# Two-level products in part of the gate and value stage of a retention and SwiGLU kernel

## The chip, the cores and the metric

One core of one Trainium2 chip runs the kernel. The time is the device time of one execution in microseconds; the median of several executions is compared. Names of engines: PE is TensorE (matmuls), PEld its weight loads, DVE is VectorE, ACT is ScalarE, POOL is GpSimd, SP is SyncE, which issues nearly all transfers.

## The reference

The inputs are q, k, v of 8 batches, 8 heads, 576 positions and 64 channels, and the weights of a gated feed-forward layer for 4608 tokens with 512 channels and 1536 inner ones. All arithmetic is in float32.

```python
scores = scale * np.matmul(q, k.transpose(0, 1, 3, 2))
ret = scores * Dmat[None]                 # causal decay, gamma by head
x = np.matmul(ret, v)                     # then (B,H,S,D) -> (4608, 512)
...
xn = x / np.sqrt(np.mean(x * x, -1, keepdims=True) + 1e-06) * rms_g
g = xn @ w_gate                           # 512 -> 1536
val = xn @ w_val                          # 512 -> 1536
out = (g / (1 + np.exp(-g)) * val) @ w_out   # 1536 -> 512
```

## The kernel before

**Units.** The 4608 tokens are worked on in nine units of 512 tokens, u = 0 to 8. The first two are mixed with the reading and joining of the weights under a plan written out by hand; units 2 to 8 run in a loop at the end of the kernel. Each has a gate and value stage, in which the 12 chunks of 128 inner channels of both gate and value are formed and multiplied into `h`, and an output stage (`across`), in which `h` meets `w_out`. While a unit's gate and value stage runs, units 2 to 6 also carry the retention of the next tokens (`prepare`, `fetch`, `slot`); from unit 7 on nothing of that is left.

**Groups.** The gate and value stage has six groups, n = 0 to 5: an even n is a gate group, an odd n the value group for the same channels. A group multiplies 512 channels by 512 inner channels (4 chunks, two in the upper half of `h` and two in the lower) for 512 tokens. It does so in the manner of Strassen and Winograd, by 7 products of halves instead of 8: the generator `up` (line 693 on) forms each product as four matmuls of 128 x 128 weights against 256 tokens and yields after each. Of the seven products, the first and fourth gather in the PSUM bank x, the second in y, the third and sixth in z, the fifth and seventh in w; eight banks rotate. The sums of weights that the seven products need were formed at the start and lie in DRAM (`w_up_blocks`, seven blocks a group); the sums of x are formed on DVE by `sums_of_x` (line 611) in the output stage before. The sums of results are left to DVE: with `u2` = x + y and `u4` = u2 + z and so on, five additions a group, each with one input in PSUM. A gate group ends in four Silu on ACT, a value group in four multiplications on DVE into `h`, and in `differences` (line 781), two subtractions that the output stage needs.

**The output stage** has two levels already: 7 products, each of 7 inner products of quarters with 3 matmuls of 128 x 128 against 128 columns (line 872). Its inner sums of `h` are formed by `inner_sums` (line 817) on POOL, in the second part of the tile `vi` (`inner`) and in `sums_x`; the first ones are put on POOL's queue in group 4, the rest when the stage begins. Results are gathered in the first part of `vi` (`vec`), joined by `combine` (seven additions on POOL, line 1061) when the stage is done, and stored by `store` (eight transfers on SP's queue) in group 1 of the next unit.

**Weights.** A ring of 17408 words a partition holds the weights in turn, one piece for each group (3584 words, 1792 KB in all) and one for each output product (2688 words, 1344 KB). `refill` (line 652) sends the next pieces on SP's queue as soon as the room they want is free; `used`, which the last product of a piece calls, triggers it. All instructions of an engine run in the order in which the program writes them (`manual_schedule`); between engines only the semaphores of the data decide.

Of the kernel before, what the change touches and what calls it, by code (L numbers as in the profile page):

```python
# [10 lines left out]
F32 = mybir.dt.float32  # L11
U32 = mybir.dt.uint32
AF = mybir.ActivationFunctionType
ALU = mybir.AluOpType
P = 128
# [29 lines left out]
def kernel(  # L45
# [11 lines left out]
    nc = tc.nc  # L57
# [3 lines left out]
    NHP = H // 2  # L61
# [16 lines left out]
    assert S == U + L and NU == B + 1 and NK == 3 and NG == 3  # L78

    const = ctx.enter_context(tc.tile_pool(name="const", bufs=1))  # L80
    raw = ctx.enter_context(tc.tile_pool(name="raw", bufs=1))
    att = ctx.enter_context(tc.tile_pool(name="att", bufs=2))
    xp = ctx.enter_context(tc.tile_pool(name="xp", bufs=3))
    tmp = ctx.enter_context(tc.tile_pool(name="tmp", bufs=4))
    PS = bass.MemoryType.PSUM
    dram = ctx.enter_context(tc.tile_pool(name="dram", bufs=1, space=bass.MemoryType.DRAM))
    banks = ctx.enter_context(tc.tile_pool(name="banks", bufs=8, space=PS))

    def bank(name):
        return banks.tile([P, 512], F32, tag="b", name=name)  # L90
# [4 lines left out]
    def row(name):  # L95
        return tmp.tile([P, U], F32, tag="n", name=name, bufs=3)
# [443 lines left out]
    def same_rows():  # L540

        t = tmp.tile([P, SQ], F32, tag="d", name="d", bufs=1)
        nc.vector.tensor_reduce(
            out=t, in_=ident.rearrange("p (a b) -> p b a", b=SQ), axis=mybir.AxisListType.X,
            op=ALU.add,
        )
        nc.vector.tensor_copy(
            out=alike.rearrange("p (a b) -> p a b", b=SQ),
            in_=t.unsqueeze(1).to_broadcast([P, P // SQ, SQ]),
        )  # L550
# [73 lines left out]

    UP, OUT = 7 * 2 * 2 * P, 7 * NK * P
    w_up_d = dram.tile([2 * NG, P, UP], F32, name="w_up_blocks")
    w_out_d = dram.tile([7, NK, P, 7 * P], F32, name="w_out_blocks")
    FIRST_ORDER = (A11, S4, A12, S1, S2, S3, A22)  # L630
# [7 lines left out]
    pieces = [("out", 0, n) for n in range(7)] + [("out", 1, n) for n in range(4, 7)]  # L638
    N_FIRST = len(pieces)
    for u in range(2, NU):  # L640
        pieces += [("up", u, n) for n in range(2 * NG)] + [("out", u, n) for n in range(7)]
    places = []
    at = AT_SUMS
    for kind, u, n in pieces:
        size = UP if kind == "up" else OUT
        if at + size > RING:
            at = AT_SETS if kind == "out" and u < 2 else 0
        places.append((at, at + size))
        at += size
    n_sent = n_used = 0  # L650

    def refill(most=len(pieces)):

        nonlocal n_sent
        while n_sent < min(most, len(pieces)):
            a, z = places[n_sent]
            kind, u, n = pieces[n_sent]
            if any(a < y and x < z for x, y in places[n_used:n_sent]):
                return
            if u > 1 and n_used < N_FIRST and a < NF * U:  # L660
                return
            o = ring[:, a:z]
            if kind == "up":
                src = w_up_d[n]
            else:
                o = o.rearrange("p (c x) -> p c x", c=NK)
                src = w_out_d[order_of(u)[n]].rearrange("c p x -> p c x")
            nc.sync.dma_start(out=o, in_=src)
            n_sent += 1

    def piece(kind, u, n):
        if kind == "out" and u == 1 and n < 4:
            i = pieces.index(("out", 0, n + 3))
        else:
            i = pieces.index((kind, u, n))
        assert i < n_sent and (i == n_used or kind == "out" and u == 0)
        a, z = places[i]
        if kind == "up":
            return ring[:, a:z].rearrange("p (b c f) -> p b c f", b=7, c=2)
        return ring[:, a:z].rearrange("p (c n d) -> p n c d", n=7, c=NK)  # L680

    def used():
        nonlocal n_used
        n_used += 1
        refill()
# [7 lines left out]
    def up(u, n):  # L693


        m, f = n % 2, n // 2 * 2
        w = piece("up", u, n)

        def product(blk, ps, start):
            for i in range(2):  # L700
                for c in range(2):
                    nc.tensor.matmul(  # L702
                        ps[:, i * HU : i * HU + HU], lhsT=w[:, PLACE[blk], c, i * P : i * P + P],
                        rhs=t_of[u][blk][:, c], start=(start and i == c == 0), stop=False,
                        skip_group_check=True,
                    )
# [36 lines left out]
        result(f, 1, "c12", u2, z)  # L743
        yield
        product(A22, w_, False)
        used()
        result(f + NH, 0, "c21", u2, w_)
        if m:
            differences(u, f)
        yield  # L750

    def up_plain(u, k, n):
# [28 lines left out]
    def differences(u, f):  # L781

        hh = h_1 if u == 1 else h
        b11, b12, b22 = hh[:, f : f + 2, :HU], hh[:, f : f + 2, HU:], hh[:, NH + f : NH + f + 2, HU:]
        for o, a, b in ((t1_of(u)[:, f : f + 2], b12, b11), (b12, b22, b12)):
            nc.vector.tensor_tensor(out=o, in0=a, in1=b, op=ALU.subtract)
# [52 lines left out]
    def across(u):  # L839
# [148 lines left out]
        for n, nm in enumerate(banks_in_turn):  # L988
# [66 lines left out]
                if n in ahead:  # L1055
                    inner_sums(u, ahead[n])
            yield
        if u and not last:
            combine(slice(0, 4), nc.gpsimd)

    def combine(b, eng=nc.vector, late=False):
# [273 lines left out]

    with tc.manual_schedule():
        start()
        for u in range(2, NU):  # L1340
            j0 = NHP * (u + 1)
            more = u + 1 < B
            for n in range(2 * NG):
                for i, _ in enumerate(up(u, n)):
                    if n == 1 and i == 4:
                        store(u - 1)
                    if n == 2 * NG - 2 and i == 1:
                        inner_sums(u, 0, 0)
                        inner_sums(u, 1, 0)
                    if more and i == 2 and 0 < n <= NHP:  # L1350
                        if j0 + n < len(jobs):
                            prepare(j0 + n)
                            fetch(j0 + n + 1)
                    if u + 1 < NU and n == 2 * NG - 1:
                        if i < NHP:
                            gather(u + 1, i, square(u + 1, i))
                        elif i == NHP:
                            fold(u + 1)
                        elif i == 6:
                            meet(u + 1)  # L1360
                    if (u, n, i) == (2, 2, 1):
                        same_rows()
                    if more and (n, i) == (NHP, 5) and j0 + NHP == len(jobs):
                        values(j0 + NHP - 1)
                if more and n <= NHP and (n or u == 2):
                    if j0 + n < len(jobs):
                        slot(j0 + n, rest=(n > 0))
                    else:
                        carried(j0 + n - 1)
            for i, _ in enumerate(across(u)):  # L1370
                if u + 1 == NU:
                    continue
                if i == 2:
                    root(u + 1)
                elif i in (3, 4, 5, 6):
                    scale_x(u + 1, (i - 3,))
                elif i == 8:
                    sums_of_x(u + 1)
# [27 lines left out]
```

## Time and profile before

| | |
|---|---|
| median of 3 runs | 1101.41 us (1101.27 to 1105.15) |
| profiled execution | 1100.22 us, its span 1098.4 us |
| TensorE clock granted | 0.997 of full speed |
| busy in the span: PE, DVE, POOL, ACT | 99%, 66%, 40%, 30% |
| gate and value stage of unit 7, of unit 8 | 883.25 to 955.90, 988.82 to 1061.35 |
| output stage of unit 7 | 955.90 to 988.82 |
| ring loads: 1792 KB, 1344 KB, issue to landing | 7.7 us, 6.4 us (medians) |
| HBM | 220 GB/s over the span |

Times inside the execution count from the start of the span. In rows of groups the first number is the summed busy time and the second the mean of one in ns; "idle before" is how long the engine stood still before such instructions, and what ended that. A matmul of float32 appears as two records.

### The profile page before, as it was taken

What the parts mean: (1) busy time and instruction counts of PE and PEld (TensorE: products, weight loads), DVE (VectorE), ACT (ScalarE), POOL (GpSimd) and SP (SyncE); (2) the same over time, 40 slices, a digit from 0 to 9 for tenths busy, and PEclk for the clock granted to TensorE, in tenths of its full rate; (3) what the DMA queues carried; (4) which work ended last, traced back from release to release, by engine and by line L of the source; (5) the groups of instructions that cost most, each with busy time, mean ns of one, the idle gap of its engine ahead of it and who ended that gap; (6) DMA issues with size and microseconds to landing.
All of it is one profiled execution on the core that took longest, in us unless ns stands there. A gap on an engine that the chain in (4) does not pass through costs nothing.

```text
span 1098.4 us, 24471 instructions
## 1 busy us (share of the span) xinstructions
PE 1085.5 (99%) x10102; PEld 912.2 (83%) x10102; DVE 727.2 (66%) x1251; ACT 328.2 (30%) x739; POOL 443.8 (40%) x421
## 2 busy tenths in 40 slices
PE   9899999999999999999999999999999999999998
PEld 7744444479988899889988998899888988998898
DVE  3878468877866774677667855677565735674467
ACT  5755564331124412332034203330233111201110
POOL 0026326538430195027702571237321932383236
PEclk9999999999999999999999999999999999999999
DMA  8756787596978876797678865888475755585471
GB/s 210 178 190 235 297 252 214 194 354 176 292 276 226 221 256 225 185 240 241 245 217 200 290 257 148 243 255 291 136 204 198 280 194 174 195 287 160 146 250 42
DMA packets 253871, 243.60 MB, mean 222 GB/s; under 512 B 193216, under 2 KB 213824, under 8 KB 247616
## 3 DMA queue, kind: packets, MB, share of 16 engines
q1 hardware_dynamic: 252320, 241.64, 69.7%
q8 instruction: 79, 1.29, 0.5%
q10 hardware_dynamic: 1440, 0.40, 0.2%
q14 instruction: 32, 0.26, 0.1%
HBM read 211.92 MB, written 30.08 MB: 220 GB/s over the span
## 4 chain that ended last, share of the span: by engine, by line
PE 97%; DVE 1%; issue 1%; ACT 0%; POOL 0%; POOLq 0%; DVEq 0%; ACTq 0%
PE up L762 15%; PE x L702 14%; PE w L702 13%; PE z L702 13%; PE y L702 7%; PE xo L872 6%; PE xp L872 4%; PE zo L872 4%; PE zp L872 3%; PE wo L872 2%; PE yo L872 2%; PE av L382 2%; PE av L402 2%; PE wp L872 2%; PE s L295 2%; PE yp L872 2%
## 5 line engine op out<-in xcount | busy, mean ns | idle before, releaser
L762 PE MATMUL up<-x,ring 128*128 128x512 f32 x384 | 167.1, 594 | 0.0
L702 PE MATMUL x<-x,ring 128*128 128x256 f32 x672 | 161.0, 382 | 0.0
L702 PE MATMUL w<-sums,ring 128*128 128x256 f32 x672 | 158.9, 379 | 0.0
L702 PE MATMUL z<-x,ring 128*128 128x256 f32 x672 | 158.7, 379 | 0.0
L824 POOL TENSOR_TENSOR vi<-h 128x384 f32<-128x384 f32 x32 | 42.4, 1326 | 275.9 <-DVE h L721 266.4
L762 PEld LDWEIGHTS up<-x,ring 128*128 128x128 f32 x384 | 72.2, 190 | 89.3 <-issue 84.7
L702 PEld LDWEIGHTS z<-x,ring 128*128 128x128 f32 x672 | 127.7, 190 | 17.4
L702 PEld LDWEIGHTS w<-sums,ring 128*128 128x128 f32 x672 | 127.6, 190 | 17.4
L702 PEld LDWEIGHTS x<-x,ring 128*128 128x128 f32 x672 | 125.3, 190 | 17.5 <-ACT m L728 0.2
L829 POOL TENSOR_TENSOR vi<-h 128x384 f32<-128x384 f32 (+2 forms) x46 | 43.9, 954 | 149.2 <-DVE h L721 149.2
L1068 POOL TENSOR_TENSOR vi<-vi 128x512 f32<-128x512 f32 (+1 forms) x77 | 78.2, 1028 | 51.9 <-DVE vi L899 35.5
L702 PE MATMUL y<-sums,ring 128*128 128x256 f32 x336 | 79.4, 379 | 0.0
L728 ACT COPY m<-x 128x512 f32<-128x512 f32 x42 | 24.6, 587 | 173.3 <-PE x L702 173.3
L709 DVE TENSOR_TENSOR h<-u,w 128x512 f32<-128x512 f32 x42 | 28.9, 688 | 67.8 <-PE w L702 67.8
L702 PEld LDWEIGHTS y<-sums,ring 128*128 128x128 f32 x336 | 63.8, 190 | 8.7
L709 DVE TENSOR_TENSOR u<-m,y 128x512 f32<-128x512 f32 x42 | 28.8, 686 | 63.2 <-PE y L702 62.5
L723 ACT ACTIVATE h<-h 128x512 f32<-128x512 f32 x63 | 39.7, 629 | 83.3 <-DVE h L709 83.3
L1188 POOL TENSOR_TENSOR vi<-vi 128x512 f32<-128x512 f32 (+1 forms) x24 | 40.7, 1696 | 30.4 <-DVE vi L1177 16.9
L709 DVE TENSOR_TENSOR u<-u,z 128x512 f32<-128x512 f32 x42 | 28.9, 687 | 33.6 <-PE z L702 33.4
L1188 POOL TENSOR_TENSOR ring<-ring 128x512 f32<-128x512 f32 x24 | 30.4, 1273 | 49.6 <-DMA w_up_blocks<-ring 43.9
L426 ACT COPY x<-av 128x192 f32<-128x192 f32 (+6 forms) x136 | 37.8, 278 | 30.0 <-PE av L402 28.5
L829 POOL TENSOR_TENSOR vi<-h,vi 128x384 f32<-128x384 f32 (+2 forms) x46 | 44.5, 968 | 3.6
(327 smaller groups left out, 2039.2 us busy)
## 6 DMA issues: line engine op xcount, KB each, us to landing
ring<-w_out_blocks SPq DMA_DIRECT2D x59, 1344.0 KB, 6.4
ring<-w_up_blocks SPq DMA_DIRECT2D x42, 1792.0 KB, 7.7
w_out_blocks<-vi SPq DMA_DIRECT2D x21, 448.0 KB, 6.2
out_dram<-vi SPq DMA_DIRECT2D x64, 128.0 KB, 3.1
qraw<-in_q_dram SPq DMA_DIRECT2D x96, 72.0 KB, 4.7
kraw<-in_k_dram SPq DMA_DIRECT2D x96, 72.0 KB, 2.7
k<-in_k_dram SPq DMA_DIRECT2D x48, 128.0 KB, 2.8
v<-in_v_dram SPq DMA_DIRECT2D x48, 128.0 KB, 3.1
```

What stands on the lines that cost most here:

```text
L295: nc.tensor.matmul(s[e][side(odd), i * L : i * L + L], lhsT=d["kT"][side(e), c * L : c * L + L], rhs=d["qT"][side(e), c * L : c * L + L], ...
L426: nc.scalar.copy(out=o, in_=part)
L702: nc.tensor.matmul(ps[:, i * HU : i * HU + HU], lhsT=w[:, PLACE[blk], c, i * P : i * P + P], rhs=t_of[u][blk][:, c], start=(start and i == ...
L709: nc.vector.tensor_tensor(out=o, in0=a, in1=pairs_of(ps), op=ALU.add)
L723: nc.scalar.activation(out=o, in_=c, func=AF.Silu)
L728: nc.scalar.copy(out=s1, in_=pairs_of(x_))
L762: nc.tensor.matmul(ps, lhsT=w[:, PLACE[blk], c % 2, i * P : i * P + P], rhs=x_of[u][:, c], start=(c == 0), stop=(c == NHP - 1),)
L824: eng.tensor_tensor(out=i1, in0=x12, in1=x11, op=ALU.subtract)
L829: eng.tensor_tensor(out=o[:, c], in0=a[:, c], in1=b[:, c], op=op)
L872: nc.tensor.matmul(ps, lhsT=lhs[:, c], rhs=w[:, s, c], start=((nm, s // 4) not in first), stop=False, skip_group_check=True,)
L1068: eng.tensor_tensor(out=t[:, :, o], in0=t[:, :, x], in1=t[:, :, y], op=ALU.add)
L1188: nc.gpsimd.tensor_tensor(out=t[o], in0=t[x], in1=t[y], op=op)
```

## The change

In the last two units (`LATE`, u = 7 and 8), groups n = 1, 2 and 3 (`DEEP`, "groups 2 to 4" counted from one) use two levels: `up_deep` takes each of the seven products apart into seven products of quarters, 49 matmuls of 128 x 128 weights against 128 tokens instead of 28 against 256. Such a product needs two banks, so a group uses all eight. The inner sums of weights are formed by `inner_blocks` on POOL, one group in each of units 3, 4 and 5, from the piece that lies in the ring, and stored by seven transfers to the new DRAM tensor `w_in_blocks`; `saves` spreads these over SP's queue. In units 7 and 8 these groups load both tensors, in two pieces a group (`HALVES`, 4096 and 3072 words) and three transfers a piece. The inner sums of x are formed on DVE in group 0 by `inner_x` (eight operations). The sums of products are kept as seven parts (`deep_c`), joined by `combine_in` (seven operations of 512 elements on POOL) after the group, and only then multiplied or put through Silu: these ends are kept in `unfinished` and run in the next groups, those of group 3 in groups 4 and 5 (`FINISH`). The pools of the retention are closed in unit 7, and `deep_c` takes their room.

Other things move: in units 7 and 8 `combine` of the unit before is written in group 1 instead of at the end of its output stage, and `store` in group 2 instead of group 1; the first `inner_sums` of units 3 to 8 are written in group 5 instead of group 4, after all saves.

```diff
-    raw = ctx.enter_context(tc.tile_pool(name="raw", bufs=1))
-    att = ctx.enter_context(tc.tile_pool(name="att", bufs=2))
     xp = ctx.enter_context(tc.tile_pool(name="xp", bufs=3))
     tmp = ctx.enter_context(tc.tile_pool(name="tmp", bufs=4))
+    retention = ctx.enter_context(ExitStack())
+    raw = retention.enter_context(tc.tile_pool(name="raw", bufs=1))
+    att = retention.enter_context(tc.tile_pool(name="att", bufs=2))
...
-    UP, OUT = 7 * 2 * 2 * P, 7 * NK * P
+    UP, OUT, IN = 7 * 2 * 2 * P, 7 * NK * P, 7 * P
+    HALVES = (0, 4), (4, 7)
+    DEEP = range(1, 4)
+    LATE = (NU - 2, NU - 1)
+    IN_ORDER = (A11, S1, S2, S3, A12, A22, S4)
+    USED_IN = (A11, S2, S1, S3), (A12, S4, A22)
...
+    assert NHP * (LATE[0] + 1) >= len(jobs)
+    w_in_d = dram.tile([len(DEEP), P, 7 * 4 * P], F32, name="w_in_blocks")
...
-        pieces += [("up", u, n) for n in range(2 * NG)] + [("out", u, n) for n in range(7)]
+        for n in range(2 * NG):
+            if u in LATE and n in DEEP:
+                pieces += [("in", u, (n, i)) for i in range(2)]
+            else:
+                pieces.append(("up", u, n))
+        pieces += [("out", u, n) for n in range(7)]
...
-        size = UP if kind == "up" else OUT
+        size = {"up": UP, "out": OUT}.get(kind)
+        if kind == "in":
+            size = (HALVES[n[1]][1] - HALVES[n[1]][0]) * 8 * P
...
+            elif kind == "in":
+                i, z = HALVES[n[1]]
+                o = o.rearrange("p (b k x) -> p b k x", k=2, x=4 * P)
+                src = w_up_d[n[0]].rearrange("p (b x) -> p b x", b=7)
+                for x, y in spans_of(IN_ORDER[i:z]):
+                    nc.sync.dma_start(
+                        out=o[:, x : x + len(y), 0], in_=src[:, y[0] : y[0] + len(y)]
+                    )
+                src = w_in_d[n[0] - DEEP[0]].rearrange("p (b x) -> p b x", b=7)[:, i:z]
+                o = o[:, :, 1]
...
+    PARTS = (A12, S4, A22, S3, A11, S2, S1)
+    ENDS = (0, 0), (1, 1), (0, 1), (1, 0)
+    deep_u = [
+        vi[:, NV + i * IN : NV + i * IN + IN].rearrange("p (s t) -> p s t", s=7) for i in range(2)
+    ]
...
+    def inner_blocks(u, n):
+        w = piece("up", u, n).rearrange("p b c f -> p b (c f)")
+        d = w_in_d[n - DEEP[0]]
+        t6 = vi[:, NV : NV + 6 * 4 * P].rearrange("p (b s f) -> p b s f", b=6, s=4)
+        t1_ = row(f"inner_{n}").rearrange("p (b s f) -> p b s f", b=1, s=4)
+        for t, b in ((t6, slice(0, 6)), (t1_, slice(6, 7))):
+            a11, a21, a12, a22 = (w[:, b, i * P : i * P + P] for i in range(4))
+            s1, s2, s3, s4 = (t[:, :, i] for i in range(4))
+            for o, x, y, op in (
+                (s3, a11, a21, ALU.subtract), (s1, a21, a22, ALU.add),
+                (s2, s1, a11, ALU.subtract), (s4, a12, s2, ALU.subtract),
+            ):
+                nc.gpsimd.tensor_tensor(out=o, in0=x, in1=y, op=op)
+        def save(i):
+            b = PLACE[IN_ORDER[i]]
+            t = t6[:, b] if b < 6 else t1_[:, 0]
+            nc.sync.dma_start(
+                out=d[:, i * 4 * P : i * 4 * P + 4 * P], in_=t.rearrange("p s f -> p (s f)")
+            )
+        saves.extend(lambda i=i: save(i) for i in range(7))
...
+    def inner_x(u, part):
+        if not deep_x1:
+            retention.close()
+            late = ctx.enter_context(tc.tile_pool(name="late", bufs=1))
+            deep_c.extend(late.tile([P, 4, 7, P], F32, name=f"deep_c_{i}") for i in range(2))
+            deep_x2.append(late.tile([P, 4, 3, P], F32, name="deep_x2"))
+            deep_x1.append(
+                xp.tile([P, NHP, U], F32, tag="x", name="inner_x")
+                .rearrange("p k (a t h) -> p k a t h", a=2, t=2)
+            )
+        x = x_of[u].rearrange("p (a c) (t s h) -> p c s a t h", c=2, t=2, s=2)
+        y = sums_x.rearrange("p i c (s h) -> p c s i h", s=2)
+        for o, v_ in (((deep_x1[0], x), (deep_x2[0], y))[part],):
+            t1_, t3, t2, t4 = (o[:, i] for i in range(4))
+            x11, x12, x21, x22 = v_[:, 0, 0], v_[:, 0, 1], v_[:, 1, 0], v_[:, 1, 1]
+            for r, a, b, op in (
+                (t1_, x12, x11, ALU.subtract), (t3, x22, x12, ALU.subtract),
+                (t2, t3, x11, ALU.add), (t4, x21, t2, ALU.subtract),
+            ):
+                nc.vector.tensor_tensor(out=r, in0=a, in1=b, op=op)
...
+    def up_deep(u, n):
+        m, f = n % 2, n // 2 * 2
+        c, first = deep_c[n % 2], deep_u[n % 2]
...
+        def product(blk, nm, start):
+            half = int(blk in USED_IN[1])
+            w = piece("in", u, (n, half))[:, IN_ORDER.index(blk) - HALVES[half][0]]
+            if start:
+                held_in[nm] = bank(f"{nm}o_{u}_{n}"), bank(f"{nm}p_{u}_{n}")
+            for i, s in enumerate(PARTS):
+                nc.tensor.matmul(
+                    held_in[nm][i // 4][:, i % 4 * P : i % 4 * P + P], lhsT=w[:, IN_AT[s]],
+                    rhs=moving(blk, s), start=(start and i % 4 == 0), stop=False,
+                    skip_group_check=True,
+                )
+            if blk == USED_IN[half][-1]:
+                used()
...
+        def copy(o, nm):
+            for t, ps in halves_of(o, nm):
+                nc.scalar.copy(out=t, in_=ps)
+        def add(o, a, nm):
+            for (t, ps), (x, _) in zip(halves_of(o, nm), halves_of(a, nm)):
+                nc.vector.tensor_tensor(out=t, in0=x, in1=ps, op=ALU.add)
+        def combine_in(which):
+            at = PARTS.index
+            for o, x, y in (
+                (A12, A11, A12), (A11, A11, S2), (S1, A11, S1), (S4, S1, S4), (A11, A11, S3),
+                (S3, S1, S3), (A22, A11, A22),
+            ):
+                nc.gpsimd.tensor_tensor(
+                    out=c[:, which, at(o)], in0=c[:, which, at(x)], in1=c[:, which, at(y)],
+                    op=ALU.add,
+                )
+        def result(i):
+            a, t = ENDS[i]
+            o = h[:, f + a * NH : f + a * NH + 2, t * HU : t * HU + HU]
+            x = c[:, i, :4].rearrange("p s t -> p (s t)").rearrange("p (f t) -> p f t", f=2)
+            if m:
+                nc.vector.tensor_tensor(out=o, in0=o, in1=x, op=ALU.mult)
+            else:
+                nc.scalar.activation(out=o, in_=x, func=AF.Silu)
...
+        def finish(n_=1):
+            for _ in range(max(0, min(n_, len(unfinished)))):
+                unfinished.pop(0)()
+        product(A11, "x", True)
+        copy(first, "x")
+        yield
+        product(S2, "y", True)
+        add(first, first, "y")
+        if m:
+            finish(len(unfinished) - 4)
+        yield
+        product(S1, "z", True)
+        add(c[:, C22], first, "z")
+        yield
+        product(S3, "w", True)
+        add(c[:, C22], c[:, C22], "w")
+        yield
+        product(A12, "x", False)
+        copy(c[:, C11], "x")
+        if m:
+            finish(len(unfinished))
+        split = n == DEEP[-1] and not m
+        if split:
+            combine_in(slice(0, 2))
+        yield
+        product(S4, "z", False)
+        add(c[:, C12], first, "z")
+        if not m:
+            finish()
+        yield
+        product(A22, "w", False)
+        add(c[:, C21], first, "w")
+        if not m:
+            finish()
+        combine_in(slice(2 * split, 4))
+        ends = [lambda i=i: result(i) for i in range(4)]
+        if m:
+            ends[:2] = [lambda: (result(C11), result(C22))]
+            ends[1:] = [lambda: (result(C12), result(C21)), lambda: differences(u, f)]
+        unfinished.extend(ends)
         yield
...
-        if u and not last:
+        if u and not last and u + 1 not in LATE:
             combine(slice(0, 4), nc.gpsimd)
...
+    z = DEEP[-1]
+    FINISH = {(z + 1, 5): 1, (z + 1, 6): 1, (z + 2, 1): 1} if z % 2 else {(z + 1, 1): 3, (z + 1, 4): 2}
...
-                for i, _ in enumerate(up(u, n)):
-                    if n == 1 and i == 4:
+                deep = u in LATE and n in DEEP
+                if u == n + 2 and n in DEEP:
+                    inner_blocks(u, n)
+                for i, _ in enumerate((up_deep if deep else up)(u, n)):
+                    if saves and (n > NHP - 1 or i % 2) and (u != n + 2 or i > 4):
+                        saves.pop(0)()
+                    if u in LATE and n == 0 and i in (0, 2):
+                        inner_x(u, i // 2)
+                    if u in LATE and (n, i) == (1, 0):
+                        combine(slice(0, 4), nc.gpsimd)
+                    if i == 4 and n == (2 if u in LATE else 1):
                         store(u - 1)
-                    if n == 2 * NG - 2 and i == 1:
+                    if (n, i) == ((2 * NG - 1, 2) if u >= DEEP[0] + 2 else (2 * NG - 2, 1)):
+                        while saves:
+                            saves.pop(0)()
                         inner_sums(u, 0, 0)
                         inner_sums(u, 1, 0)
...
+                    for _ in range(FINISH.get((n, i), 0) if u in LATE else 0):
+                        unfinished.pop(0)()
...
```

More of the change, by code (lines that the diff above doesn't have):

```diff
@@ L623, in sums_of_x, with spans_of @@
         t_of[u] = {A11: b11, A12: b21, S1: b12, A22: t4, S2: t2, S3: t3, S4: b22}
-    UP, OUT = 7 * 2 * 2 * P, 7 * NK * P
+    UP, OUT, IN = 7 * 2 * 2 * P, 7 * NK * P, 7 * P
[4 more added lines that the diff above has]
+    USED_IN = (A11, S2, S1, S3), (A12, S4, A22)
+    def spans_of(blocks):
+        spans = []
+        for i, b in enumerate(blocks):
+            if spans and spans[-1][1][-1] + 1 == PLACE[b]:
+                spans[-1][1].append(PLACE[b])
+            else:
+                spans.append((i, [PLACE[b]]))
+        return spans
+    assert NHP * (LATE[0] + 1) >= len(jobs)
+    w_in_d = dram.tile([len(DEEP), P, 7 * 4 * P], F32, name="w_in_blocks")
     w_up_d = dram.tile([2 * NG, P, UP], F32, name="w_up_blocks")
@@ L679, in piece @@
             return ring[:, a:z].rearrange("p (b c f) -> p b c f", b=7, c=2)
+        if kind == "in":
+            return ring[:, a:z].rearrange("p (b s f) -> p b s f", s=8, f=P)
         return ring[:, a:z].rearrange("p (c n d) -> p n c d", n=7, c=NK)
@@ L749, in up @@
             differences(u, f)
+        yield
+    PARTS = (A12, S4, A22, S3, A11, S2, S1)
+    ENDS = (0, 0), (1, 1), (0, 1), (1, 0)
+    C11, C22, C12, C21 = range(4)
+    deep_c = []
+    deep_x2 = []
+    deep_u = [
+        vi[:, NV + i * IN : NV + i * IN + IN].rearrange("p (s t) -> p s t", s=7) for i in range(2)
+    ]
+    deep_x1 = []
+    unfinished, saves = [], []
+    IN_AT = {A11: 0, A12: 2, A22: 3, S1: 4, S2: 5, S3: 6, S4: 7}
+    def inner_blocks(u, n):
[18 more added lines that the diff above has]
+        saves.extend(lambda i=i: save(i) for i in range(7))
@@ new lines, in up_deep, with moving, halves_of @@
+    def up_deep(u, n):
+        m, f = n % 2, n // 2 * 2
+        c, first = deep_c[n % 2], deep_u[n % 2]
+        held_in = {}
+        def moving(blk, s):
+            x = t_of[u][blk]
+            plain = {A11: (0, 0), A12: (1, 0), S4: (1, 1)}
+            if s in plain:
+                i, t = plain[s]
+                return x[:, i, t * P : t * P + P]
+            kind = {S1: 0, S3: 1, S2: 2, A22: 3}[s]
+            if blk in (S2, S3, A22):
+                return deep_x2[0][:, kind, (S2, S3, A22).index(blk)]
+            return deep_x1[0][:, kind, int(blk in (A12, S4)), int(blk in (S1, S4))]
+        def product(blk, nm, start):
[11 more added lines that the diff above has]
+                used()
+        def halves_of(t, nm):
+            a, b = held_in[nm]
+            return (
+                (t[:, :4].rearrange("p s t -> p (s t)"), a),
+                (t[:, 4:].rearrange("p s t -> p (s t)"), b[:, : 3 * P]),
+            )
[14 more added lines that the diff above has]
+                    op=ALU.add,
+                )
+        def result(i):
[4 more added lines that the diff above has]
+                nc.vector.tensor_tensor(out=o, in0=o, in1=x, op=ALU.mult)
+            else:
+                nc.scalar.activation(out=o, in_=x, func=AF.Silu)
[28 more added lines that the diff above has]
+            finish()
+        yield
+        product(A22, "w", False)
[8 more added lines that the diff above has]
+        unfinished.extend(ends)
@@ L1369 @@
                         carried(j0 + n - 1)
+            assert not unfinished and not saves
             for i, _ in enumerate(across(u)):
```

## The prediction

> **What bounds the kernel now.** I read the page's chain of waits first, then the same chain piece by piece in the last two units, then the windows of busy time by group there, then the transfers, and last VectorE (DVE) and GpSimd (POOL) in order of time. From the page:
>
> ```profile
> PE 97%; DVE 1%; issue 1%; ACT 0%; POOL 0%; POOLq 0%; DVEq 0%; ACTq 0%
> ...
> L1068 POOL TENSOR_TENSOR vi<-vi 128x512 f32<-128x512 f32 (+1 forms) x77 | 78.2, 1028 | 51.9 <-DVE vi L899 35.5
> ...
> L1188 POOL TENSOR_TENSOR vi<-vi 128x896 f32<-128x896 f32 x12 | 25.4, 2119 | 0.9
> ...
> ring<-w_out_blocks SPq DMA_DIRECT2D x59, 1344.0 KB, 6.4
> ring<-w_up_blocks SPq DMA_DIRECT2D x42, 1792.0 KB, 7.7
> ```
>
> TensorE (PE) sets the end: 97% of the chain is its own work, and idle time of the others costs nothing until it stops PE. The chain in unit 7 has no gap (start, length, what):
>
> ```profile
> 893.61 1.73 PE w L702 x8
> 895.34 1.73 PE x L702 x8
> ...
> 955.90 1.43 PE xo L872 x12
> 958.67 1.34 PE xp L872 x12
> 960.68 1.34 PE zo L872 x12
> ```
>
> A matmul of f32 is two records, so x8 is one product of four matmuls over 256 columns: 1.727 us, 216 ns a record. L872 shows what a matmul over 128 columns costs: 1.34/12 = 112 ns a record. Windows (length, then PE, PEld, DVE, ACT, POOL busy) for groups 0, 1, 3 and the output products of unit 7:
>
> ```profile
> 883.25:895.34 12.09, 12.09 (x57) 10.64 (x57) 3.90 (x6) 2.44 (x4) 8.80 (x7) 1.00 0.41 153
> 895.34:907.42 12.08, 12.08 (x57) 10.63 (x57) 5.51 (x8) 1.22 (x2) 0.00 (x0) 1.00 0.80 239
> 919.51:931.60 12.09, 12.09 (x58) 10.64 (x57) 5.84 (x8) 1.22 (x2) 4.22 (x6) 1.00 0.35 114
> 955.90:988.82 32.92, 32.92 (x295) 32.92 (x296) 24.87 (x32) 2.91 (x6) 27.63 (x25) 1.00 0.80 283
> ```
>
> A group is 7 products, 12.09 us; DVE is under half busy there, POOL nearly idle outside the combine (8.80). Last, two kinds of DVE operation beside a busy POOL, and alone:
>
> ```profile
> 868.69 1.48 DVE L621 TENSOR_TENSOR sums<-x 128x512 f32<-128x512 f32 x1
> 870.20 1.37 DVE L621 TENSOR_TENSOR sums<-sums,x 128x512 f32<-128x512 f32 x1
> 883.34 0.69 DVE L899 TENSOR_TENSOR vi<-vi,xo 128x512 f32<-128x512 f32 x1 [2.53 <-PE xo L872]
> 883.95 0.55 DVE L899 TENSOR_TENSOR vi<-vi,xp 128x384 f32<-128x384 f32 x1
> 908.79 0.69 DVE L786 TENSOR_TENSOR t<-h 128x512 f32<-128x512 f32 x1
> 869.58 1.44 POOL L829 TENSOR_TENSOR vi<-h 128x384 f32<-128x384 f32 x1
> 884.11 9.11 POOL L1068 TENSOR_TENSOR vi<-vi 128x512 f32<-128x512 f32 x7 [5.02 <-DVE vi L899]
> ```
>
> An operation with both inputs in SBUF takes 0.69 us alone (L786, POOL idle) and up to 1.48 beside POOL (L621); POOL's 384-wide one goes from 1.00 (the one at 865.08) to 1.44. A DVE operation with one input in PSUM keeps its 0.69 (L709 during the combine of 884.11 to 893.22).
>
> **PE, the gain.** In units 7 and 8, groups 1 to 3 go from 7 x 4 matmuls of 256 columns (56 records, 12.09 us) to 7 x 7 of 128 (98 records). At L872's rate over a whole stage, 294 records in 32.92 us, or 111.7 ns between its products (42 records in 4.69), that is 98 x 0.1117 = 10.95 us: 1.14 less a group, **6.9 us** for six. The trace has no quarter product of this kind. Bounds: half a 256-column record, 108 ns, gives 10.58 and 9.1 us in all; the first twelve of a stage (1.43/12 = 119 ns) give 11.68 and 2.5 us. I take L872's: same tile shapes, same weights-per-matmul ratio.
>
> **VectorE, the price.** A deep group has five additions of 7 quarters, each 0.69 + 0.55 = 1.24 (L899's pair): 6.2 us of DVE in 10.95. POOL joins the quarters with 7 operations of 512, 9.1 us (L1068's 9.11). The ends of a value group then run late, in the next groups, beside that join. Follow group 2, its start at 0, product steps of 1.56. Group 1's last addition ends at 0.6, its join at 9.8. Group 2's sixth addition ends at 10.0, then two multiplications for group 1 with POOL idle: 11.3. The seventh ends at 12.5 and starts the next join, which lasts past 21. In its shade DVE has two more multiplications, an addition of group 3 (1.24), two differences, then the addition that reads bank z (first part 0.69). With 0.69 each for the four SBUF-only ones z is read at 17.4, with 1.48 at 20.4. PE writes z again at group 3's sixth product, 10.95 + 7.82 = 18.8. So between nothing and 1.6 us a unit. I take 1.25 for each operation, nearer to the contended end since POOL runs throughout: z is read at 19.4, 0.65 late, **+1.3 us** for both units (0 to 3.3). What is late next, the second banks and w, stays inside that stall; ACT's four Silu wait for the join too and delay group 4's first copy by under a microsecond, which x needs only 5 us later.
>
> [...] The trace's worst case is 1.48, with the two engines taking turns, and some overlapped ones stay at 0.69 to 0.9, so I stay with the rows.
>
> Group 0 gets eight more DVE operations for the quarter sums of x. They start at 884.5, beside the combine: 4 x 1.48 = 5.9, then two additions, 891.8, then four of 384 at 3/4 of that, 896.2. The third matmul of group 1's second product wants the last of them at 897.35. Slack 1.1; with 1.48 for the narrow ones too, 0.35 late per unit. I count nothing. Writing the combine later (group 1) changes POOL's order not at all, since POOL has nothing else queued in group 0; it still starts when DVE's last output addition ends. The store of the unit before, moved to group 2, is 8 transfers on SP's queue behind loads already sent.
>
> **Loads.** A deep group needs 7168 words a partition, 3.67 MB, instead of 1.84, in six transfers on SP's queue instead of one (some 0.33 us of issue each, SP is free there). From the two rows of ring loads: 0.459 MB more take 1.3 us more, so 353 GB/s and 2.5 us fixed. The ring has 17408 words. Laying the pieces out in it, each with that rate and its moment of release, every piece of unit 7 lands at least 6 us early. In unit 8 both halves of group 2 can only be sent when group 0 is done: 2.10 MB land 5.9 + 2.5 = 8.4 us later and are wanted after 10.95, slack 2.5; the halves of group 3 keep about 3. Over that stretch 2 x 3.67 + 1.84 = 9.2 MB are due in 3 x 10.95 us less 2.5, 302 GB/s; 5 us windows of output stages show 341 and 360. Counted at nothing; this cover is the thinnest.
>
> **Units 3 to 5.** Each forms one group's inner sums: on POOL 4 operations of 768 (by the slope from 512 at 1274 ns to 896 at 2119, 1.84 us) and 4 of 128 (0.61), 9.8 us, where POOL otherwise sits idle for 34 to 39 us of each unit; the ring piece it reads is held no longer than by PE. Its transfers: 7 stores of 256 KB, 2.3 us of SP issue. They stand ahead of unit u+1's head loads on that queue and behind those of the same group; in unit 5 the last two wait behind loads that held SP from 715.4 to 726.1, so land near 729.5, and the inner sums of the output products, which overwrite that room and were moved to group 5, end their first part near 733.5 where the second part now starts at 731.0. PE wants the result at 737.5 and later: 2.5 us late out of some 5 in hand. Nothing, up to 1 us if DVE slows.
>
> **Sum.** 6.9 - 1.3 = 5.6 us. Against the profiled execution: 1100.22 (span 1098.4 and 1.8 around it) becomes 1094.6. The median of the three runs is 1101.41, 1.2 above the profiled one; taken from it, **1095.8**. What a measurement can tell from no change is about 0.5%, 5.5 us, so the forecast sits on that line.
>
> **Rivals.** (1) *VectorE stops PE longer*: the four shaded operations and the quarter sums of x come at their contended ends, 1.6 + 0.35 a unit, 3.9 us, and the matmuls after each bank change cost a little more; gain 1 to 4 us, about 1098.5. For: L621 doubles beside POOL. Against: L721 beside small POOL operations stays at 0.7 to 0.9. (2) *The ring runs dry*, slower than before: transfers in rows of 2 KB and split in three, beside 1 MB of stores, move at the page's mean of 220 GB/s. Then unit 8 has its 9.2 MB after 41.7 + 2.5 = 44.2 us instead of 32.9, 11.3 late, and unit 7, with one more group in hand, about half of that: 17 - 6.9, some 1111. It decides where the lateness passes 12.4 us, below about 235 GB/s. Against: 1792 KB in 7.7 us is 238 even with the fixed part in it, and PE never waited for a load. (3) *Quarter products cost no less*: at 123 ns a record the gain is zero, 1101. Against: L872 at 112 over seven stages.
>
> **Chances.** Forecast (gain 4 to 7.5, 1094 to 1097.5) 0.65, of which 0.48 lies past the 5.5 us; rival 1 0.18, rival 2 0.10, rival 3 and costs in units 3 to 5 0.07. Faster 0.48, within 0.40, slower 0.12 (rival 2, and 0.02 of the last). The range, 1093.5 to 1102, takes in the forecast and rivals 1 and 3, and leaves out rival 2 and gains above 8 us.
>
> **What will show it.** Right: groups 1 to 3 of units 7 and 8 last 10.9 to 11.1 us, and a gap of some 0.6 us before group 3's sixth product is released by DVE. Rival 1: gaps over 1.5 us there, or one at group 1's second product behind the sums of x. Rival 2: PE released by a ring load in unit 8, groups 2 to 4. Rival 3: records over 118 ns with no releaser. Wrong altogether: new gaps in units 3 to 5, or at the start of an output stage.

## The result, and the profile after

The changed kernel takes 1108.54 us (median of 9 runs, 1106.16 to 1111.76), the kernel before 1101.78 beside it (9 runs): a ratio of 1.006, with a 95% interval of 1.0044 to 1.0075. It is 6.8 us slower, where 5.6 us faster was forecast, and outside the forecast range. The profiled execution of the changed kernel has a span of 1104.9 us, against 1098.4. The ratios below leave out one execution of the first experiment, which took 2874.56 us for a reason that nothing here shows.

The page's chain of waits, engines' shares, and the new join of quarter sums among its groups:

```profile
PE 94%; DVE 2%; issue 1%; ACT 1%; POOL 1%; SPq 1%; DMA 0%; POOLq 0%; DVEq 0%; ACTq 0%
...
L903 POOL TENSOR_TENSOR deep_c<-deep_c 128x512 f32<-128x512 f32 x42 | 55.4, 1333 | 40.5 <-DVE deep_c L895 21.0
```

PE's share fell from 97% to 94%. DVE's rose from 1% to 2%, and ACT, POOL and SP's queue, which had rounded to 0%, now have 1% each. The windows (length, then PE, PEld, DVE, ACT, POOL busy, clock granted, DMA share, GB/s) of groups 0, 1 and 3 of unit 7, then of group 0 of unit 8, say where:

```profile
887.31:904.77 17.46, 14.12 (x58) 11.53 (x57) 14.17 (x14) 2.41 (x4) 10.54 (x7) 0.91 0.38 135
904.77:915.72 10.95, 10.95 (x99) 10.95 (x98) 6.04 (x10) 2.62 (x5) 0.00 (x0) 0.99 0.81 276
...
926.84:937.82 10.98, 10.98 (x99) 10.98 (x99) 10.72 (x16) 2.13 (x4) 9.23 (x7) 1.00 0.94 294
...
995.04:1011.01 15.97, 12.63 (x59) 10.48 (x58) 14.17 (x14) 2.41 (x4) 10.54 (x7) 1.00 0.60 196
```

The two-level groups do what they should: about 10.95 us with PE busy throughout, where a group took 12.09. (The second window ends 0.17 us before group 1 does. Group 1 took 11.12 us, since the clock was still low when it began.) Group 0, which is computed as before, grew from 12.09 to 17.46 and 15.97 us. Between the two profiles, stage by stage:

| stage | before | after | difference |
|---|---|---|---|
| unit 3, group 4, from the start of the first product to that of the fourth | 5.38 | 7.15 | +1.8 |
| unit 5, from group 5 to the end of the output stage | 45.33 | 47.55 | +2.2 |
| unit 7, group 0 | 12.09 | 17.46 | +5.4 |
| unit 7, groups 1 to 3 | 36.26 | 33.05 | -3.2 |
| unit 8, group 0 | 12.09 | 15.97 | +3.9 |
| unit 8, groups 1 to 3 | 36.26 | 32.88 | -3.4 |
| sum | | | +6.7 (spans: +6.5) |

So 6.6 us were won and 13.3 lost, at four places. The chain in group 0 of unit 7 (start, length, what; "issue" is time in which the engine waited for nothing that the profile shows):

```profile
894.94 0.69 DVE u L747
...
896.32 3.13 DVE deep_x L848 x2
...
900.54 0.69 DVE h L747
...
901.28 3.49 PE w L740 x8
904.77 1.07 PE xo L874 x8
```

PE waits for `h L747`, the addition that reads bank w, before its last product may gather there. The fifth product, whose result it reads, and the addition before it were done by 896.40, but it stood in DVE's queue behind the last four sums of x and ran at 900.54. DVE in order of time, and POOL's line beside it:

```profile
888.48 3.19 DVE L848 TENSOR_TENSOR inner_x<-x 128x512 f32<-128x512 f32 x2
891.70 1.64 DVE L848 TENSOR_TENSOR inner_x<-inner_x,x 128x512 f32<-128x512 f32 x1
...
896.32 3.12 DVE L848 TENSOR_TENSOR deep_x<-sums 128x384 f32<-128x384 f32 x2
899.48 0.56 DVE L848 TENSOR_TENSOR deep_x<-deep_x,sums 128x384 f32<-128x384 f32 x1
...
888.17 10.85 POOL L1276 TENSOR_TENSOR vi<-vi 128x512 f32<-128x512 f32 x7 [5.04 <-DVE vi L1107]
```

While POOL joins the last unit's results (888.17 to 899.02, 10.85 us instead of 9.11), a sum of x takes 1.6 us whether it has 512 elements or 384; after 899 the 384-wide ones take 0.56. And the join starts at 888.17, released by one of DVE's last output additions (L1107), although the program writes it in group 1.

### The profile page after: what moved, and what is told of

It is laid out like the page before. It is cut to its first block, busy times and chain, and to the rows that moved or that the text cites. A ratio compares the mean times of both kernels' runs of the same rounds, so it can differ in the third digit from the quotient of the medians.

```text
span 1104.9 us, 25234 instructions
## 1 busy us (share of the span) xinstructions
PE 1082.0 (98%) x10354; PEld 914.4 (83%) x10354; DVE 763.3 (69%) x1297; ACT 336.1 (30%) x757; POOL 526.3 (48%) x487
## 4 chain that ended last, share of the span: by engine, by line
PE 94%; DVE 2%; issue 1%; ACT 1%; POOL 1%; SPq 1%; DMA 0%; POOLq 0%; DVEq 0%; ACTq 0%
PE up L970 15%; PE x L740 11%; PE w L740 11%; PE z L740 11%; PE xo L1080 6%; PE y L740 5%; PE xp L1080 4%; PE zo L1080 4%; PE zp L1080 3%; PE wo L1080 2%; PE yo L1080 2%; PE av L383 2%; PE wp L1080 2%; PE av L403 2%; PE s L296 2%; PE yp L1080 2%
## 5 line engine op out<-in xcount | busy, mean ns | idle before, releaser
L740 PE MATMUL w<-sums,ring 128*128 128x256 f32 x576 | 137.9, 383 | 5.7 <-DVE h L747 5.7
L740 PE MATMUL x<-x,ring 128*128 128x256 f32 x576 | 138.5, 383 | 1.6 <-issue 1.6
L740 PE MATMUL z<-x,ring 128*128 128x256 f32 x576 | 136.3, 379 | 1.0 <-DVE u L747 1.0
L740 PEld LDWEIGHTS w<-sums,ring 128*128 128x128 f32 x576 | 110.1, 191 | 21.6 <-DVE h L747 6.5
L740 PEld LDWEIGHTS z<-x,ring 128*128 128x128 f32 x576 | 109.3, 190 | 16.6 <-DVE u L747 1.8
L740 PEld LDWEIGHTS x<-x,ring 128*128 128x128 f32 x576 | 106.9, 190 | 16.7 <-issue 1.8
L903 POOL TENSOR_TENSOR deep_c<-deep_c 128x512 f32<-128x512 f32 x42 | 55.4, 1333 | 40.5 <-DVE deep_c L895 21.0
L740 PE MATMUL y<-sums,ring 128*128 128x256 f32 x288 | 68.0, 379 | 0.0
L1037 POOL TENSOR_TENSOR vi<-vi,h 128x384 f32<-128x384 f32 (+2 forms) x46 | 43.7, 949 | 42.8 <-DMA w_in_blocks<-vi 39.5
L747 DVE TENSOR_TENSOR h<-u,w 128x512 f32<-128x512 f32 x38 | 26.1, 687 | 53.8 <-PE w L740 53.7
L740 PEld LDWEIGHTS y<-sums,ring 128*128 128x128 f32 x288 | 54.7, 190 | 7.4
L747 DVE TENSOR_TENSOR u<-m,y 128x512 f32<-128x512 f32 x36 | 24.7, 687 | 49.5 <-PE y L740 42.8
L1037 POOL TENSOR_TENSOR vi<-h,vi 128x384 f32<-128x384 f32 (+2 forms) x46 | 44.1, 959 | 10.8 <-DMA w_in_blocks<-vi 7.5
```

The lines of the kernel that those rows point to most:

```text
L740: nc.tensor.matmul(ps[:, i * HU : i * HU + HU], lhsT=w[:, PLACE[blk], c, i * P : i * P + P], rhs=t_of[u][blk][:, c], start=(start and i == ...
L903: nc.gpsimd.tensor_tensor(out=c[:, which, at(o)], in0=c[:, which, at(x)], in1=c[:, which, at(y)], op=ALU.add,)
L1037: eng.tensor_tensor(out=o[:, c], in0=a[:, c], in1=b[:, c], op=op)
```

## The experiments

Ratios are against the kernel before, run on the same chip (medians of 1102.08 us in the first four experiments and 1101.73 in the other three). Differences from the changed kernel are between medians of separate sets of runs.

### Let the join wait for the sums of x

```diff
...
+            ins = eng.tensor_tensor(out=t[:, :, o], ...)
+            if o == A12 and last_x and eng is nc.gpsimd and not late:
+                follow(ins, last_x[0])
```

> Edit: the seven joins on POOL that were moved into group 1 of units 7 and 8 now wait for the last of the eight sums of x on DVE, so the two no longer overlap; nothing else. Theory A (the eight DVE operations take 1.55 to 1.64 us each because they alternate with POOL, and PE waits within group 0 for the additions queued behind them): the operations go to 0.69 and 0.55, group 0 lasts 12.1 to 12.4 us in both units instead of 17.46 and 15.97, no clock drop, and the time falls by 7.5 to 9.3 us, to 1099 to 1101. Rival B (the eight operations are too much for DVE in group 0 even alone, 8 x 0.62 = 5 us in a queue whose additions PE waits for): group 0 stays above 13.5 us and the gain is under 5 us. Rival C (the late join delays the joins of the deep groups or the store, and PE waits there instead): group 0 is short, but groups 2 to 4 grow by over 1 us.

Measured 1099.45 us, ratio 0.9977 (0.9963 to 0.9991), 9.1 below the changed kernel. Group 0 of unit 7 as a window, then DVE and POOL in it:

```profile
887.16:899.25 12.09, 12.09 (x59) 10.64 (x58) 8.46 (x14) 2.45 (x4) 3.77 (x3) 1.00 0.57 195
```

```profile
888.32 1.29 DVE L849 TENSOR_TENSOR inner_x<-x 128x512 f32<-128x512 f32 x2
...
895.33 9.13 POOL L1277 TENSOR_TENSOR vi<-vi 128x512 f32<-128x512 f32 x7 [12.32 <-DVE deep_x L849]
```

Theory A holds, and B falls: alone, the eight operations fit into group 0 without a wait (unit 8's group 0 lasts 12.09 us too). C falls too: the join, now from 895.33 on, delays nothing, and groups 1 to 3 last 10.94 to 11.01 us.

### The sums of weights alone

`LATE = ()`: the last two units as before, units 3 to 5 with the block sums and stores.

> Edit: the last two units as in the kernel before (no two-level groups, joins and stores at their old places); the inner sums of weights in units 3 to 5, their stores and the moved first inner sums of the output stage stay. It shows what units 3 to 5 cost alone. Theory A (the last two stores of unit 5 stand behind loads on SP's queue, and POOL's inner sums wait for them): 2.3 us slower than before, all at the start of unit 5's output stage, and up to 1.8 us more if the gap of 1.62 us in unit 3, for which the trace names no releaser, belongs to the stores too: 1103.5 to 1106. Rival (the lateness comes from the two last units alone, and these two gaps were chance): within 1 us of before.

Measured 1106.50 us, ratio 1.0041 (1.0027 to 1.0055), 4.4 us slower: a third of all that was lost comes from the preparation in units 3 to 5. Group 4's first product in unit 3 runs through in the kernel before (first line), stops after its third record in the changed kernel (second line), and does so again here (the others):

```profile
477.64 1.93 PE x L702 x8
...
478.58 1.62 issue
...
479.52 2.40 issue
...
483.44 3.13 PE y L739 x8
```

In this execution, the slowest of the six, the gap is longer, and the product after it runs at half speed (3.13 us instead of 1.73): 4.3 us are lost in unit 3, 0.8 in unit 4 and 2.8 in unit 5's output stage. The changed kernel shows what holds that stage:

```profile
732.27 0.61 SPq L210
...
732.93 0.58 SPq L821
...
733.56 2.54 DMA w_in_blocks<-vi
...
736.24 0.46 POOL vi L1037
...
741.42 1.51 PE xp L1080 x10
```

The store L821 is issued when SP has come through the loads of group 4 (L210 is the last), lands at 736.1, and only then may POOL write its inner sums over that room. PE stands still for 0.98 us before it gets them, is 1.5 us late at the next product, and loses another 0.7 at three later ones of the stage.

### The stores ahead of the loads

```diff
+                    while saves and (n, i) == (NHP, 1):
+                        saves.pop(0)()
```

> Edit: in group 4 all stores of weight sums that are left are sent at its second step, ahead of the loads of q, k and v of that group; the rest as in the changed kernel. Theory A: POOL's inner sums in unit 5 no longer wait for a store, its output stage lasts 32.9 us from the first product on instead of some 35.2, and the time falls by 2.3 us from the changed kernel's 1108.5, to about 1106. Rival (the inner sums are late because they were moved to group 5, not because of the stores): unit 5's output stage still stands still for over 1 us, and the time stays above 1107.5.

Measured 1106.87 us, ratio 1.0042 (1.0029 to 1.0056), 1.7 below the changed kernel; the medians alone would hardly settle it. The window of unit 5's output stage does:

```profile
741.55:774.47 32.92, 32.92 (x296) 32.92 (x296) 25.62 (x33) 2.92 (x6) 29.03 (x26) 1.00 0.95 363
```

It lasts 32.92 us as before, with the inner sums still written in group 5. So the stores were the cause, not the moved sums.

### Both repairs

> Edits of the two others together (the join waits for the sums of x; the stores go ahead of the loads). If the two losses are separate they add up: 9.8 to 11.6 us below the changed kernel, 1097 to 1099, and 3 to 5 us below the kernel before, since the 6.6 us that the two-level groups save are then left, less up to 1.8 us for the unexplained gap in unit 3. If they hang together (the same lateness counted twice), the gain over the better of the two single edits is under 1 us.

Measured 1096.99 us, ratio 0.9951 (0.9937 to 0.9965): 11.6 below the changed kernel, 5.1 below the kernel before. The two repairs alone gave 9.1 and 1.7, 10.8 together; within the noise the losses add up, so they are separate. The gap in unit 3 is still there, 1.07 us in this profile.

### Other units for the sums of weights

`u == n + 3` in place of `u == n + 2`, on top of both repairs.

> Edit: the version with both repairs (join after the sums of x, stores ahead of the loads), and in addition the inner sums of weights formed and stored in units 4, 5 and 6 instead of 3, 4 and 5. Theory A (the gap of 1.1 to 2.4 us on PE in unit 3, which every kernel with the stores shows and the kernel before does not, comes from the stores: they crowd the transfers just when PE's next instructions have to be fetched): unit 3 has no gap over 0.3 us, and the time falls by about 1 us from the version with both repairs (1096.99), to about 1096, if no fetch in units 4 to 6 is hit in its place. Rival (the gap comes from the longer program, whose instructions lie differently, not from the stores): the gap stays in unit 3 at over 1 us.

Measured 1096.00 us, ratio 0.9947 (0.9928 to 0.9966). The chain at the matmul in question:

```profile
478.23 1.06 PE x L740 x4
479.29 0.08 issue
```

Without stores in unit 3 the gap is 0.08 us, against 0.95 to 2.40 in the six profiles of kernels that store there. In return PE loses 0.3 us in unit 5. The rival, the layout of the program, falls by this profile; by time this version and the last can't be told apart. It has the lowest median of all, 0.5% below the kernel before.

### No stores

As the block sums alone, without `saves.extend(...)`.

> Edit: as the run with the block sums alone (last two units as before), but the sums of weights are not stored: POOL forms them, nothing goes to memory. What is left out is the seven transfers in each of units 3 to 5; nothing reads them here. Theory A (all that units 3 to 5 cost comes from the stores, by SP's queue in unit 5 and by crowding in units 3 and 4): the gaps in units 3 and 5 vanish and the time is that of the kernel before within 0.5 us, against 4.4 us more with the stores. [...]

Measured 1102.49 us against 1101.73, ratio 1.0012 (0.9998 to 1.0026). The chain has neither gap (group 4 of unit 3 runs on with 0.24 us lost). The 0.8 us that the medians differ by are more than the half microsecond expected, but the interval reaches from 0.2 us faster to 2.9 slower, so the time alone does not rule out that POOL's own sums, or the later place of the first inner sums, cost over 2 us. The profile does: its execution is 3.9 us longer than the one profiled before, but PE is 3.7 us behind already when unit 3 starts and 3.9 when the last output stage does, so units 3 to 8 lost only 0.2. POOL's own sums cost little, if anything. PE's program is the same as in the run with the stores, so the gap in unit 3 comes from the transfers.

### The overlap kept, the order changed

```diff
-                    if u in LATE and n == 0 and i in (0, 2):
-                        inner_x(u, i // 2)
+                    if u in LATE and n == 0 and i in (0, 5):
+                        inner_x(u, int(i > 0))
```

(with the stores ahead of the loads)

> Edit: stores ahead of the loads as before, but the join on POOL does not wait for the sums of x: it overlaps them as in the changed kernel. Instead the second four sums of x stand later in DVE's queue, after group 0's sixth product, so that the additions that read banks z and w come ahead of them. Theory A in its first form (the overlap with POOL is what costs): the first four sums still take 1.55 to 1.64 us each, group 0 stays above 15 us, the time above 1104. Theory A' (the overlap only matters through what is queued behind it; PE waits for the reader of bank w): group 0 shrinks to about 12.6 us, with one wait of 0.5 us left for bank z behind the first four, and the time comes to 1097.5 to 1098.5, half a microsecond per unit above the version in which nothing overlaps.

Measured 1097.85 us, ratio 0.9962 (0.9949 to 0.9976). Group 0 of unit 7, and DVE in it:

```profile
888.66:901.53 12.87, 12.36 (x59) 10.57 (x58) 11.13 (x12) 2.45 (x4) 10.23 (x7) 1.00 0.57 183
```

```profile
893.05 1.64 DVE L848 TENSOR_TENSOR inner_x<-inner_x,x 128x512 f32<-128x512 f32 x1
...
897.86 0.69 DVE L747 TENSOR_TENSOR h<-u,w 128x512 f32<-128x512 f32 x1
```

The first four sums are as slow as ever, yet PE loses 0.78 us a unit instead of 3.9 to 5.4, since the reader of w now runs at 897.86, ahead of the last four. Here only the first four sums overlap the join; the last four, at 900.51, have it behind them and take 0.5 us each. So the overlap alone costs 0.78 us a unit, through the addition that reads bank z behind those first four; what made it 3.9 to 5.4 was the place of the last four in the queue.

## Why the prediction was wrong, point by point

**PE's gain** held: 10.95 us a group was worked out, 10.94 to 11.12 came, 6.6 us in all instead of 6.9. The bounds of 108 and 119 ns a record were not needed.

**The price on DVE after the joins** was placed rightly and sized too high: 0.65 us a unit for bank z in group 3, of which 0.04 and 0.06 came. The two multiplications beside the join took 2.37 us together and the two differences 2.34, close to the 1.25 each that was assumed, but the chain ran ahead of the working, partly since one operation began some 0.1 us before the last one ended: z was read 18.5 us after the start of group 2 instead of 19.4. That is at 934.37, and PE wrote there again from 934.49 on. It is a margin of nothing, not a safe one.

**The step that failed** is the one on group 0: "I count nothing". The eight operations were weighed against the one who needs their results, group 1's second product at 897.35, and not against what stands behind them in DVE's queue. The same working had all that was needed: the last sum ends at 896.2, the addition behind it would then read bank w by 896.9, and group 0's own seventh product wanted that bank at 893.6. That is 3.3 us late in each unit, 6.6 in all, enough to turn the forecast from faster to no gain. Measured: 0.51 us at bank z and 2.83 at bank w, in both units, and in unit 7 another 1.8 for the last product at half the clock. The two groups grew by 9.3 us in all, and letting the join wait gave 9.1 back.

**Its size** was off as well: a 384-wide sum beside POOL was put at 1.11 us, scaled by its width, and took 1.58 and 1.62. The first operations of the two engines, one by one, show what they wait for:

```profile
888.17 1.27 POOL L1276 TENSOR_TENSOR vi<-vi 128x512 f32<-128x512 f32 x1 [5.04 <-DVE vi L1107]
888.48 1.52 DVE L848 TENSOR_TENSOR inner_x<-x 128x512 f32<-128x512 f32 x1
889.52 1.59 POOL L1276 TENSOR_TENSOR vi<-vi 128x512 f32<-128x512 f32 x1
889.92 1.75 DVE L848 TENSOR_TENSOR inner_x<-x 128x512 f32<-128x512 f32 x1
```

POOL's first ends at 889.44, DVE's some 0.55 us later, POOL's second 1.1 after that, DVE's second 0.55 after that, and so on; the 384-wide sums end 0.41 after POOL's. So here each lasts as long as what is left of the other engine's operation, plus its own part: 1.52, 1.59 and 1.75 us after POOL's first. The two additions with a PSUM input that ran beside the join (894.94 and 895.72) kept 0.68 and 0.69. And 1.48 was not the worst case of the kernel before: beside 896-wide operations of POOL (213.96 to 216.04, 216.12 to 218.53) two 512-wide ones of DVE took longer.

```profile
214.44 2.15 DVE L786 TENSOR_TENSOR t<-h 128x512 f32<-128x512 f32 x1
216.62 2.45 DVE L786 TENSOR_TENSOR h<-h 128x512 f32<-128x512 f32 x1
```

**Units 3 to 5** were put at "nothing, up to 1 us" and cost 4.4. The danger was named, stores behind the loads of the same group; its size was not. SP came to them at 732.9, not 726.1, so they landed at 736.1 and not 729.5. Of these 6.8 us, 1.9 are the delay with which all of unit 5 starts, nearly all of it unit 3's gap. Four stores that SP sends ahead of group 4's loads (from 718.02 on) held it for 2.0. Those loads then held it 12.2 us instead of 10.7; whether the added transfers slow them was not tried. The gap in unit 3 was not foreseen at all.

**What held**: the ring loads never stopped PE in unit 8, so the rival of the dry ring, which held most of the chance of slower, is not what happened; and writing the join later did not move it, as said. None of the rivals named what happened in group 0: rival 1 looked for the sums of x at group 1's second product, and at 0.35 us a unit. Costs in units 3 to 5 had a share of 0.07 in the chances, and new gaps there were among the signs of being wrong, but the sum had them at nothing.

Together: 9.3 us in group 0, 4.0 in units 3 and 5 and 0.3 less gain, against 1.2 us that bank z did not cost, make the 12.4 us between 5.6 faster and 6.8 slower.

## What to carry to other kernels

When operations are added to an engine that runs in order, ask two questions: when is the result needed, and what is queued behind them, and who waits for that. If two engines take turns on two-input operations, as DVE and POOL did here, price each at what is left of the other's operation plus its own part; its own width then counts for little (1.6 us with 512 elements and with 384). Writing the join later in the program did not delay it (it began at 888.17, still in group 0), since its own queue had nothing before it; where an instruction must not overlap, give it a dependency. And work done ahead in otherwise idle engines still has transfers, whose place in the queue is part of its price.

## What the runs showed of the hardware beyond that

**The clock.** After the wait of 2.83 us in unit 7 the granted clock fell to half for 3.41 us, from 901.61 to 905.02; after the same wait in unit 8 it did not. The last product of group 0 took 3.49 us there and 1.99 in unit 8: there the wait of 2.83 us cost another 1.5. The profile with the stores ahead of the loads repeats it (17.50 and 15.95 us for the two groups), and so does the slow product after the 2.40 us gap above. In the profiles of the kernel before and of the changed kernel, the changes of the clock lie whole multiples of 3.413 us apart (from 34.62 to 1096.16 us in the first, 311 of them; from 905.02 to 1103.00 in the second, 58). So the time can be cut into windows of that length, counted on from one change. Two neighbours in unit 7 of the changed kernel, two in unit 8, and two in unit 3 of the run with the sums of weights alone (length, PE busy second, clock third from the right):

```profile
898.20:901.61 3.41, 0.58 (x4) 0.31 (x3) 3.34 (x5) 0.35 (x1) 0.82 (x1) 1.00 0.00 0
901.61:905.02 3.41, 3.41 (x11) 2.78 (x10) 0.42 (x2) 0.88 (x2) 0.00 (x0) 0.50 0.02 2
...
1004.01:1007.42 3.41, 1.99 (x8) 1.44 (x8) 3.38 (x4) 0.00 (x0) 2.75 (x2) 1.00 0.57 192
1007.42:1010.83 3.41, 1.82 (x8) 1.63 (x9) 2.10 (x4) 1.23 (x2) 0.00 (x0) 1.00 0.00 0
...
479.33:482.74 3.41, 1.01 (x5) 0.74 (x5) 2.74 (x10) 1.06 (x4) 0.29 (x1) 1.00 0.58 100
482.75:486.16 3.41, 3.41 (x9) 2.71 (x9) 0.00 (x0) 1.44 (x3) 0.15 (x1) 0.50 0.61 99
```

In unit 7 the whole wait fell into one window, and PE was busy for 0.58 us of it; the next window ran at half. In unit 8 the border of two windows cut the wait, PE was busy for over 1.8 us in each, and the clock held. Between 280 and 1090 us, the chains of the nine profiles have a product at half speed three times: the two of 3.49 and 3.13 us behind these windows, with PE busy for 0.58 and 1.01 us, and one of 3.54 with the stores ahead of the loads. In the kernel before and the changed kernel no window of that stretch with 1.79 us or more was followed by a fall (1.79 is that of 478.36 to 481.77, around the gap in unit 3); nothing measured here lies between 1.01 and 1.79. So the length of the wait alone does not tell: the same 2.83 us brought the clock down in unit 7 and not in unit 8, and in unit 3 a window idle for 70% was enough.

**The gap in unit 3.** It begins in all six profiles of kernels that store there after the third record of the same product, with no wait for another engine, just after a stretch in which the transfers ran at 372 GB/s (477 to 478 us in the changed kernel; the gap begins at 478.58). That the stores bring it on is shown by the run without them. What PE waits for is not named. That it is its next instructions is an estimate, from a queue of packets of 16 KB whose number goes with PE's records (`q8 instruction`, one packet for some 256 records of matmuls and weight loads: 79 for 20204 in the kernel before, 81 for 20708 in the changed one). In the changed kernel a packet ends at 478.49, just before the gap, and PE goes on 1.71 us after that end. Four of the six profiles have a second such gap in unit 4, of 0.13 to 0.58 us. In the kernel before, the packet ended at 476.26, 2.2 us before PE came to that place, and PE ran on. The packet at the gap takes no longer (0.89 us, 1.16 in the kernel before). It starts later: 1.0 us before PE comes to the place, 3.4 in the kernel before. Why it starts later beside the stores was not tried.
